# Windowed attention and a two-layer network in split float32: q's and k's parts made over 128 rows and copied into place, the weights' halves added in one step

## The chip, the cores and the metric

The kernel runs on one core of a Trainium2 chip. A core has five engines that run side by side, each with its own queue of instructions: TensorE (PE in the profile; its weight loads are a row of their own, PEld), VectorE (DVE), ScalarE (ACT), GpSimd (POOL) and SyncE (SP), which here only issues DMA transfers. TensorE multiplies a stationary operand, loaded by a weight load, with a moving operand and adds into a bank of PSUM; the other operands lie in SBUF, 128 rows (partitions) wide. The metric is the device time of one execution in microseconds (us), median of several.

## What is computed

The inputs are q, k and v of 8 batches, 8 heads, 576 positions and 64 numbers a head. Each position attends to itself and the 127 positions before it, with a bias that falls with the distance by a slope that depends on the head. The result, 4608 rows of 512, goes through two matrices with a piecewise quadratic function between them. q and k are drawn as normal numbers times 0.8, v times 0.1.

```python
scores = scale * np.matmul(q, k.transpose(0, 1, 3, 2))
rel = pos[:, None] - pos[None, :]
bias = slopes[:, None, None] * (-np.abs(rel))[None, :, :]
mask = (rel >= 0) & (rel < 128)
scores = np.where(mask, scores + bias[None], -1000000000.0)
attn = np.exp(scores - np.max(scores, axis=-1, keepdims=True))
attn = attn / (np.sum(attn, axis=-1, keepdims=True) + 1e-09)
x = np.matmul(attn, v)                       # heads side by side: 4608 x 512
h = x @ w_in                                 # 512 x 2048
g = np.where(h >= 1, h, np.where(h <= -1, 0.0, (h + 1) ** 2 / 4))
out = g @ w_out                              # 2048 x 512
```

## The kernel before

**Split numbers.** Most matmuls run on float32r, a form of float32 with fewer bits. A number is split in two parts: its float32r rounding (high) and the rest (low), and a product is made as high by high, low by high and high by low, all added in one PSUM bank. The copy that rounds is ScalarE's, the subtraction that gives the rest is VectorE's (GpSimd's in the network).

**Chunks, pairs and heads.** The 4608 rows are 12 chunks of 384 (three blocks of 128). In a chunk the 8 heads are taken as 4 pairs, since q and k lie transposed in HBM with two heads of 64 rows on 128 partitions. In the code p counts pairs (48 in all), m heads (96), c chunks. Chunks 0 and 1 are "light" (`LIGHT = 2`): their attention is in plain float32, without splits, and a score is one matmul over the 64 rows of its head (line 288).

**From chunk 2 on.** For a pair, `prepare_k` and `prepare_q` make the operands of the scores. The stationary operand `ql[:, j]` of head j holds q's high part on the head's own 64 rows and its low part on the other 64 (`o_hi`, `o_lo` in lines 241 to 243; one ScalarE and one VectorE step of 64 rows for each head). For that, k's high part must stand on both halves of the rows: `load_qk` brings each head's k from HBM twice, one DMA for each half (line 215), and `prepare_k` splits the doubled k into `kk` (high, line 252) and `kl` (low, line 253), of 128 rows by 2 heads by up to 512 positions. A block of scores is then two matmuls: line 290 multiplies q's high and low parts with k's high part, line 291 the same weights with k's low part, over all 128 rows.

**Softmax.** VectorE adds the table of distances and finds the maximum (line 294), ScalarE takes the exponential and the sum (line 296), VectorE adds up the sums and inverts them (302, 303). A row of scores spans two blocks of keys, 256 wide, of which every column of the left half is masked where the same column of the right half is not; so the two halves are added into 128 columns and multiplied by the inverse in one step for each block (line 309; line 307 where there is no left block). TensorE transposes the 128x128 weights (318). `weights_t` splits them (328, 329), GpSimd parts them again by a triangular mask into the two blocks (331, 333), and `values` multiplies with v's parts (383) and adds up (384 to 387).

**The network.** `layer1` multiplies one of 16 slices of `w_in` with the chunk's x, 12 matmuls of 384 columns into one bank (lines 408 to 410), which ScalarE (417) and VectorE (418, 419) turn into g, split by ScalarE (426) and GpSimd (427). `layer2` follows two slices later with 9 matmuls of 512 columns (441 to 443; 438 in chunk 0, unsplit). The weights arrive as 64-bit floats and are turned into float32 on the chip during the first chunk.

**What sets the order.** The program writes out, step by step, pieces of the attention of chunk c+1 between the steps of the network of chunk c (`segments`, `emit_attention`). A planner then orders every engine's instructions by this order and by its own estimates of when each is ready, places the buffers and makes the waits; each engine works through its queue in that order. Loads of q, k and v, and stores of the output, are issued in order on SP. Most attention buffers exist once (`ql`, `kk`, `kl`, `kr`, `qr`, `z`), so a pair's operands are made after the scores of the pair before it; the weights `ep` exist twice.

Of the kernel before, what the change touches and what calls it, by code (L numbers as in the profile page):

```python
# [8 lines left out]
F32 = mybir.dt.float32  # L9
F32R = mybir.dt.float32r  # L10
I32 = mybir.dt.int32
U32 = mybir.dt.uint32
AF = mybir.ActivationFunctionType
ALU = mybir.AluOpType
# [4 lines left out]
def windowed_attention_then_ffn(  # L19
# [21 lines left out]
    V, S, G, T, DMA = nc.vector, nc.scalar, nc.gpsimd, nc.tensor, nc.sync  # L41

    H, SEQ, D = 8, 576, 64
    NT, DM = out.shape
    DFF = w_in.shape[1]
    P = 128
    NPAIR = H // 2
# [3 lines left out]
    CH = NQB * P  # L51
# [8 lines left out]
    LIGHT = 2  # L60
# [4 lines left out]
    ap1 = ctx.enter_context(tc.tile_pool(name="ap1", bufs=1))  # L65
# [24 lines left out]
    qscale = const.tile([P, NPAIR], F32, name="qscale")  # L90
# [78 lines left out]
    pair = {}  # L169
    head = {}  # L170
    xn = {}
    last_x = [None]
    done_t = {}
    lo_rows = [slice(0, D), slice(D, P)]
    hi_rows = [slice(D, P), slice(0, D)]

    def before(c):

        return 0 if c % CYCLE == 0 else 1

    def load_first(p):

        n = f"_{p}"
        if p == 0:
            qq = [ap1.tile([P, CH], F32, name="qr" + n, tag="qr"), ap1.tile([P, 2, CH], F32, name="ql" + n, tag="ql")[:, 0]]
            kv = [ap1.tile([P, CH + P], F32, name="kr" + n, tag="kr")[:, :CH], ap1.tile([P, CH], F32, name="vn" + n, tag="vn")]
        elif p == 1:
            t = ap1.tile([P, 2, CH], F32, name="qq" + n, tag="kl")
            qq = [t[:, 0], t[:, 1]]
            kv = [ap1.tile([P, CH], F32, name="kr" + n, tag="kk"), ap1.tile([P, CH], F32, name="vn" + n, tag="vs")]  # L190
        else:
            t = wp.tile([P, 2, CH], F32, name="qq" + n, tag=f"wi{NFC - NPAIR + p}")
            qq = [t[:, 0], t[:, 1]]
            t = wp.tile([P, 2, CH], F32, name="kv" + n, tag=f"wo{NFC - NPAIR + p}")
            kv = [t[:, 0], t[:, 1]]
        vn = kv[1].rearrange("p (i j d) -> p i j d", j=2, d=D)
        pair[p] = dict(qr=qq[0], ql=qq[1].rearrange("p (o t) -> p o t", o=1), kr=kv[0].rearrange("p (o t) -> p o t", o=1), vn=vn)
        DMA.dma_start(qq[0], q[p * P:(p + 1) * P, :CH])
        DMA.dma_start(kv[0], k[p * P:(p + 1) * P, :CH])
        DMA.dma_start(vn.rearrange("p i j d -> p i (j d)"), v[:CH, p * P:(p + 1) * P].rearrange("(i p) d -> p i d", p=P))  # L200

    def load_qk(p):

        c, g = divmod(p, NPAIR)
        if c == 0:
            return
        n = CH + before(c) * P
        st = pair[p] = {}
        qr = st["qr"] = ap1.tile([P, CH], F32, name=f"qr_{p}", tag="qr")
        DMA.dma_start(qr, q[g * P:(g + 1) * P, c * CH:(c + 1) * CH])  # L210
        kr = st["kr"] = ap1.tile([P, 2, CH + P], F32, name=f"kr_{p}", tag="kk" if c < LIGHT and p % 2 else "kr")
        if c < LIGHT:
            DMA.dma_start(kr[:, 0, :n], k[g * P:(g + 1) * P, (c + 1) * CH - n:(c + 1) * CH])
            return
        for half in (slice(0, D), slice(D, P)):
            DMA.dma_start(kr[half, :, :n],
                          k[g * P:(g + 1) * P, (c + 1) * CH - n:(c + 1) * CH].rearrange("(j d) t -> d j t", j=2))

    def load_v(p):
        c, g = divmod(p, NPAIR)  # L220
# [11 lines left out]
    def prepare_q(p):  # L232
        qr = pair[p]["qr"]
        if p // NPAIR < LIGHT:
            if p >= NPAIR:
                pair[p]["ql"] = ap1.tile([P, 2, CH], F32, name=f"ql_{p}", tag="ql")
            return S.activation(pair[p]["ql"][:, 0], qr, AF.Copy, scale=qscale[:, p % NPAIR:p % NPAIR + 1])
        ql = pair[p]["ql"] = ap1.tile([P, 2, CH], F32R, name=f"ql_{p}", tag="ql")
        for j in range(2):
            scale = 2.0 ** (2 * (p % NPAIR) + j + 1) / 8.0  # L240
            o_hi, o_lo, s = ql[lo_rows[j], j], ql[hi_rows[j], j], qr[lo_rows[j]]
            S.mul(o_hi, s, scale)
            V.scalar_tensor_tensor(o_lo, s, scale, o_hi.bitcast(F32), ALU.mult, ALU.subtract)

    def prepare_k(p):
        if p // NPAIR < LIGHT:
            return
        n = CH + before(p // NPAIR) * P
        kk = pair[p]["kk"] = ap1.tile([P, 2, CH + P], F32R, name=f"kk_{p}", tag="kk")
        kl = pair[p]["kl"] = ap1.tile([P, 2, CH + P], F32R, name=f"kl_{p}", tag="kl")  # L250
        kr = pair[p]["kr"]
        S.copy(kk[:, :, :n], kr[:, :, :n])
        V.tensor_tensor(kl[:, :, :n], kr[:, :, :n], kk[:, :, :n].bitcast(F32), ALU.subtract)

    def prepare_v(p):
        if p // NPAIR < LIGHT:
# [7 lines left out]
    def scores(m, blks):  # L264
        p, j = divmod(m, 2)
        c = p // NPAIR
        ql, kr, kk, kl = (pair[p].get(x) for x in ("ql", "kr", "kk", "kl"))
        if m not in head:
            head[m] = dict(ep=ap1.tile([P, NQB, P], F32, name=f"ep_{m}", tag="ep", bufs=2),
                           z=wp.tile([P, NQB, 2 * P], F32, name=f"z_{m}", tag=f"wi{NFC - 3}") if c == 0 and j else  # L270
                           ap1.tile([P, NQB, 2 * P], F32, name=f"z_{m}", tag="z"),
                           nmax=ap1.tile([P, 4], F32, name=f"nmax_{m}", tag="nmax", bufs=2),
                           sum=sums[:, m % 2])
        st = head[m]
        nmax, sm, ep, z = st["nmax"], st["sum"], st["ep"], st["z"]
        slope = 2.0 ** -(m % H + 1)
        pt = bank(f"s_{m}_{blks[0]}").rearrange("r (m w) -> r m w", w=2 * P)
        b0 = before(c)
        win = []
        for n, i in enumerate(blks):  # L280
            lone = i + b0 == 0
            c0 = P if lone else D if c % CYCLE == 1 and i == 2 else 0
            k0 = (i + b0 - 1) * P + c0
            o = pt[:, n, c0:]
            win.append((o, c0, lone))
            if c < LIGHT:
                r, qs, ks = lo_rows[j], slice(i * P, (i + 1) * P), slice(k0, k0 + 2 * P - c0)
                st["scored"] = T.matmul(o, ql[r, 0, qs], kr[r, 0, ks], start=True, stop=True).ins  # L288
                continue
            T.matmul(o, ql[:, j, i * P:(i + 1) * P], kk[:, j, k0:k0 + 2 * P - c0], start=True, stop=False)  # L290
            T.matmul(o, ql[:, j, i * P:(i + 1) * P], kl[:, j, k0:k0 + 2 * P - c0], start=False, stop=True)  # L291
        for i, (o, c0, lone) in zip(blks, win):
            r = rel_end if c % CYCLE == 1 and i == 1 else rel
            V.tensor_tensor_reduce(out=z[:, i, c0:], in0=o, in1=r[:, c0:], op0=ALU.add, op1=ALU.min, scale=-slope,  # L294
                                   scalar=3.0e38, accum_out=nmax[:, i:i + 1])
            S.activation(z[:, i, c0:], z[:, i, c0:], AF.Exp, bias=nmax[:, i:i + 1], scale=-1.0,  # L296
                         accum_out=sm[:, i, 0:1])
        if blks[-1] == NQB - 1:
            if c % CYCLE == 1:
                G.memset(z[:, 2, :D], 0.0)  # L300
            rc = st["rc"] = ap1.tile([P, 8], F32, name=f"rc_{m}", tag="rc", bufs=2)
            V.tensor_reduce(rc[:, :NQB], sm, mybir.AxisListType.X, ALU.add)
            V.reciprocal(rc[:, :NQB], rc[:, :NQB])

            for i in range(NQB):
                if i + b0 == 0:
                    V.tensor_tensor(ep[:, i, :], z[:, i, P:], rc[:, i:i + 1].broadcast_to([P, P]), ALU.mult)
                else:
                    st["folded"] = V.tensor_tensor_reduce(out=ep[:, i, :], in0=z[:, i, :P], in1=z[:, i, P:], op0=ALU.add, op1=ALU.add,  # L309
                                           scale=rc[:, i:i + 1], scalar=0.0, accum_out=rc[:, 4 + i:5 + i])  # L310

    def weights_t(m):

# [5 lines left out]
        if m < LIGHT * H:  # L319
            own = lu[:, 0, 1::2, :].bitcast(F32)  # L320
            ga = S.copy(own, pt)
            G.affine_select(out=lu[:, 0, 0::2, :].bitcast(F32), in_=own, pattern=[[0, NQB], [-1, P]],
                            base=0, channel_multiplier=1, compare_op=ALU.is_gt, fill=0.0)
            gg = G.affine_select(out=own, in_=own, pattern=[[0, NQB], [1, P]],
                                 base=0, channel_multiplier=-1, compare_op=ALU.is_ge, fill=0.0)
            done_t[m] = [head[m]["folded"].ins, ga.ins, gg.ins]
            return
        ga = S.copy(lu[:, 0, 1::2, :], pt)
        gv = V.tensor_tensor(lu[:, 1, 1::2, :], pt, lu[:, 0, 1::2, :].bitcast(F32), ALU.subtract)  # L329
# [248 lines left out]
```

## Time and profile before

| | before |
|---|---|
| median of 3 runs | 1066.62 us (1060.73 to 1067.28) |
| the profiled execution | 1068.07 us, of which the span of the instructions is 1066.0 us |
| mean granted clock of TensorE | 0.981 of full speed |
| busy: TensorE, VectorE, ScalarE, GpSimd | 1038.2, 790.1, 618.9, 369.2 us |
| HBM read, written | 58.98 MB, 9.44 MB |

The page of the profile gives each engine's busy time, the chain of work that ended last, and groups of instructions: the line of the kernel, the engine, the operation, output<-inputs with shapes (128x384 is partitions by elements; for matmuls the rows by columns of the array that are used come first, as 64\*128), the count, then the busy time in us and the mean duration in ns, and after the bar the time that the engine stood idle before these instructions and who ended that. A row of waits has who waited for whom, the total in us, how often, and the longest. A row of the timeline has the start in us, the duration in us, the engine, the line and the operation, x the number of neighbours that were merged into it. The records of matmuls overlap: their ends are modelled.

### The profile page before, as it was taken

How to read it: one execution, taken by the hardware profiler on the slowest of the kernel's cores; microseconds unless marked ns; L12 is line 12 of the kernel's file. 1: busy time of each engine (PE TensorE's matmuls, PEld its weight loads, DVE VectorE, ACT ScalarE, POOL GpSimd, SP SyncE). 2: the span in 40 equal slices, each digit the busy share in tenths (PEclk: the TensorE clock that was granted, in tenths of full speed). 3: DMA queues.
4: the chain of work that ended last, by engine and by line, in shares of the span. 5: the costliest groups of instructions: out<-in, count | busy, mean ns of one | idle time of the engine just before them, and what ended most of it. 6: DMA issues, size and time to landing. Idle time of an engine off the chain costs nothing.

```text
span 1066.0 us, 16843 instructions
## 1 busy us (share of the span) xinstructions
PE 1038.2 (97%) x5508; PEld 906.8 (85%) x5508; DVE 790.1 (74%) x2249; ACT 618.9 (58%) x1476; POOL 369.2 (35%) x419
## 2 busy tenths in 40 slices
PE   8999999999999999999999999999999999999998
PEld 5576667998988988998998988999889889899996
DVE  6687799878877788877678887777787897863322
ACT  6687766656556556656456565555555655742322
POOL 2120004444443433433343443433333443333221
PEclk8599999999999999999999999999999999999999
DMA  8346412112212122121113112111121221200000
GB/s 284 100 164 202 136 48 67 53 40 67 65 38 67 48 65 67 41 53 60 36 48 89 43 48 65 62 30 38 60 65 38 77 65 48 67 1 1 31 1 30
DMA packets 58903, 69.50 MB, mean 65 GB/s; under 512 B 4032, under 2 KB 44480, under 8 KB 58816
## 3 DMA queue, kind: packets, MB, share of 16 engines
q1 hardware_dynamic: 48064, 51.66, 17.4%
q10 hardware_dynamic: 10752, 16.78, 4.6%
q8 instruction: 43, 0.70, 0.3%
q14 instruction: 44, 0.36, 0.1%
HBM read 58.98 MB, written 9.44 MB: 64 GB/s over the span
## 4 chain that ended last, share of the span: by engine, by line
PE 85%; DVE 6%; ACT 5%; POOL 2%; issue 2%; DMA 0%; ACTq 0%; SPq 0%; DVEq 0%; POOLq 0%
PE h L408 11%; PE h L409 11%; PE h L410 11%; PE acc L441 11%; PE acc L442 10%; PE acc L443 10%; PE x L383 5%; PE acc L438 3%; PE p L318 3%; PE s L291 2%; PE s L290 2%; PE x L359 2%; PE s L288 2%; ACT z L296 1%; POOL lu L333 1%
## 5 line engine op out<-in xcount | busy, mean ns | idle before, releaser
L427 POOL TENSOR_TENSOR gl<-g,gh 128x384 fp32r<-128x384 f32 x176 | 183.5, 1042 | 435.0 <-ACT gh L426 429.1
L408 PE MATMUL h<-xh,wi 128*128 128x384 f32 x768 | 264.8, 345 | 1.7 <-ACT sg L417 1.7
L409 PE MATMUL h<-xl,wi 128*128 128x384 f32 x768 | 259.8, 338 | 0.0
L410 PE MATMUL h<-xh,wi 128*128 128x384 f32 x768 | 259.4, 338 | 0.0
L441 PE MATMUL acc<-wo,gh 128*128 128x512 f32 x528 | 212.0, 401 | 8.1 <-ACT gh L426 8.1
L418 DVE SCALAR_TENSOR_TENSOR g<-sg 128x384 f32<-128x384 f32 x192 | 108.6, 566 | 148.4 <-ACT sg L417 136.4
L442 PE MATMUL acc<-wo,gh 128*128 128x512 f32 x528 | 208.2, 394 | 0.0
L426 ACT CAST gh<-g 128x384 fp32r<-128x384 f32 x176 | 90.3, 513 | 193.6 <-DVE g L419 179.4
L417 ACT ACTIVATE sg<-h,quarter 128x384 f32<-128x384 f32 x192 | 111.2, 579 | 140.2 <-PE h L410 139.5
L296 ACT ACTIVATE z<-z,nmax 128x256 f32<-128x256 f32 (+2 forms) x288 | 139.0, 485 | 28.5 <-DVE nmax L294 26.6
L443 PE MATMUL acc<-wo,gl 128*128 128x512 f32 x528 | 155.5, 398 | 0.0
L408 PEld LDWEIGHTS h<-xh,wi 128*128 128x128 f32 x768 | 144.6, 188 | 10.7 <-ACT sg L417 3.4
L409 PEld LDWEIGHTS h<-xl,wi 128*128 128x128 f32 x768 | 144.6, 188 | 5.9 <-issue 1.4
L410 PEld LDWEIGHTS h<-xh,wi 128*128 128x128 f32 x768 | 144.4, 188 | 0.0
L294 DVE CUSTOM_DVE_ANT_0 z<-s,rel 128x256 f32<-128x256 f32 (+2 forms) x256 | 94.4, 394 | 51.5 <-PE s L291 44.3
L309 DVE CUSTOM_DVE_ANT_0 ep<-z,rc 128x128 f32<-128x128 f32 x256 | 129.9, 548 | 1.6
L331 POOL TENSOR_SCALAR_AFFINE_SELECT lu<-lu 128x768 fp32r<-128x768 f32 x80 | 80.8, 1010 | 130.2 <-DVE lu L329 121.6
L441 PEld LDWEIGHTS acc<-wo,gh 128*128 128x128 f32 x528 | 99.4, 188 | 27.2 <-ACT gh L426 10.6
L419 DVE SCALAR_TENSOR_TENSOR g<-sg,g 128x384 f32<-128x384 f32 x192 | 112.0, 584 | 3.7
L443 PEld LDWEIGHTS acc<-wo,gl 128*128 128x128 f32 x528 | 97.1, 189 | 19.8 <-POOL gl L427 0.2
L442 PEld LDWEIGHTS acc<-wo,gh 128*128 128x128 f32 x528 | 99.5, 188 | 16.5
L333 POOL TENSOR_SCALAR_AFFINE_SELECT lu<-lu 128x768 fp32r<-128x768 f32 x80 | 81.4, 1018 | 4.6
(88 smaller groups left out, 1461.1 us busy)
## 6 DMA issues: line engine op xcount, KB each, us to landing
kr<-in_k_dram SPq DMA_DIRECT2D x60, 256.0 KB, 4.1
out_dram<-o SPq DMA_DIRECT2D x36, 256.0 KB, 2.4
qr<-in_q_dram SPq DMA_DIRECT2D x45, 192.0 KB, 3.7
rawi<-in_moe_w_in_dram ACTq DMA_DIRECT2D x16, 512.0 KB, 4.6
rawo<-in_moe_w_out_dram ACTq DMA_DIRECT2D x16, 512.0 KB, 5.6
vn<-in_v_dram SPq DMA_DIRECT2D x32, 256.0 KB, 2.8
kr<-in_k_dram SPq DMA_DIRECT2D x26, 192.0 KB, 3.4
vn<-in_v_dram SPq DMA_DIRECT2D x14, 192.0 KB, 2.5
```

The lines of the kernel that those rows point to most:

```text
L296: S.activation(z[:, i, c0:], z[:, i, c0:], AF.Exp, bias=nmax[:, i:i + 1], scale=-1.0, accum_out=sm[:, i, 0:1])
L309: st["folded"] = V.tensor_tensor_reduce(out=ep[:, i, :], in0=z[:, i, :P], in1=z[:, i, P:], op0=ALU.add, op1=ALU.add, scale=rc[:, i:i + 1], ...
L408: T.matmul(ph, wi[fc][:, 0, cc, :], xh, start=(cc == 0), stop=False)
L409: T.matmul(ph, wi[fc][:, 0, cc, :], xl, start=False, stop=False)
L410: T.matmul(ph, wi[fc][:, 1, cc, :], xh, start=False, stop=(cc == NCC - 1))
L417: first = S.activation(sg, ph, AF.Relu, bias=quarter[:, 0:1], scale=0.25)
L418: V.scalar_tensor_tensor(g, sg, 0.5, sg, ALU.min, ALU.mult)
L419: last = V.scalar_tensor_tensor(g, sg, -0.25, g, ALU.add, ALU.max)
L427: G.tensor_tensor(gl, g, gh.bitcast(F32), ALU.subtract)
L441: T.matmul(a, gh[:, ts], wo[fc][:, 0], start=first, stop=False)
L442: T.matmul(a, gh[:, ts], wo[fc][:, 1], start=False, stop=False)
L443: T.matmul(a, gl[:, ts], wo[fc][:, 0], start=False, stop=last)
```

## The change

For q: one ScalarE step multiplies all 128 rows (both heads) by their scales and rounds them into a new tile `qp`; one VectorE step makes the rest, in place of the loaded q. Four DMA copies from SBUF to SBUF, two for each head, then lay the 64-row parts out in `ql` as before.

For k: it is loaded once, in its 128 rows. ScalarE rounds it into `kp[:, 0]`, VectorE writes the rest into `kp[:, 1]`, and four DMA copies bring the high parts into `kk`, each head's on both halves of the rows. The low part stays in its own rows; the matmul of line 291 therefore takes the 64 rows of q's high part alone as its weights, and no longer multiplies q's low part with k's low part.

For the weights: VectorE adds the halves of all blocks in one step in place, and ScalarE multiplies each block by its inverse sums while it writes `ep`.

```diff
@@ load_qk @@
-        kr = st["kr"] = ap1.tile([P, 2, CH + P], F32, name=f"kr_{p}", tag="kk" if c < LIGHT and p % 2 else "kr")
-        if c < LIGHT:
-            DMA.dma_start(kr[:, 0, :n], k[g * P:(g + 1) * P, (c + 1) * CH - n:(c + 1) * CH])
-            return
-        for half in (slice(0, D), slice(D, P)):
-            DMA.dma_start(kr[half, :, :n],
-                          k[g * P:(g + 1) * P, (c + 1) * CH - n:(c + 1) * CH].rearrange("(j d) t -> d j t", j=2))
+        kr = st["kr"] = ap1.tile([P, CH + P], F32, name=f"kr_{p}", tag="kk" if c < LIGHT and p % 2 else "kr")
+        DMA.dma_start(kr[:, :n], k[g * P:(g + 1) * P, (c + 1) * CH - n:(c + 1) * CH])
@@ prepare_q @@
+        scale = qscale[:, p % NPAIR:p % NPAIR + 1]
+        qp = ap1.tile([P, CH], F32R, name=f"qp_{p}", tag="qp")
+        S.activation(qp, qr, AF.Copy, scale=scale)
+        V.scalar_tensor_tensor(qr.bitcast(F32R), qr, scale, qp.bitcast(F32), ALU.mult, ALU.subtract)
         ql = pair[p]["ql"] = ap1.tile([P, 2, CH], F32R, name=f"ql_{p}", tag="ql")
         for j in range(2):
-            scale = 2.0 ** (2 * (p % NPAIR) + j + 1) / 8.0
-            o_hi, o_lo, s = ql[lo_rows[j], j], ql[hi_rows[j], j], qr[lo_rows[j]]
-            S.mul(o_hi, s, scale)
-            V.scalar_tensor_tensor(o_lo, s, scale, o_hi.bitcast(F32), ALU.mult, ALU.subtract)
+            DMA.dma_start(ql[lo_rows[j], j].bitcast(F32), qp[lo_rows[j]].bitcast(F32))
+            DMA.dma_start(ql[hi_rows[j], j].bitcast(F32), qr[lo_rows[j]])
@@ prepare_k @@
+        kr = pair[p]["kr"]
+        kp = ap1.tile([P, 2, CH + P], F32R, name=f"kp_{p}", tag="kl")
+        S.copy(kp[:, 0, :n], kr[:, :n])
+        V.tensor_tensor(kp[:, 1, :n], kr[:, :n], kp[:, 0, :n].bitcast(F32), ALU.subtract)
+        pair[p]["kl"] = kp[:, 1]
+
         kk = pair[p]["kk"] = ap1.tile([P, 2, CH + P], F32R, name=f"kk_{p}", tag="kk")
-        kl = pair[p]["kl"] = ap1.tile([P, 2, CH + P], F32R, name=f"kl_{p}", tag="kl")
-        kr = pair[p]["kr"]
-        S.copy(kk[:, :, :n], kr[:, :, :n])
-        V.tensor_tensor(kl[:, :, :n], kr[:, :, :n], kk[:, :, :n].bitcast(F32), ALU.subtract)
+        for j in range(2):
+            for r in lo_rows:
+                DMA.dma_start(kk[r, j, :n].bitcast(F32), kp[lo_rows[j], 0, :n].bitcast(F32))
@@ scores @@
             T.matmul(o, ql[:, j, i * P:(i + 1) * P], kk[:, j, k0:k0 + 2 * P - c0], start=True, stop=False)
-            T.matmul(o, ql[:, j, i * P:(i + 1) * P], kl[:, j, k0:k0 + 2 * P - c0], start=False, stop=True)
+            T.matmul(o, ql[lo_rows[j], j, i * P:(i + 1) * P], kl[lo_rows[j], k0:k0 + 2 * P - c0], start=False, stop=True)
...
+            n0 = 1 - b0
+            f = V.tensor_tensor(z[:, n0:, P:], z[:, n0:, :P], z[:, n0:, P:], ALU.add)
             for i in range(NQB):
-                if i + b0 == 0:
-                    V.tensor_tensor(ep[:, i, :], z[:, i, P:], rc[:, i:i + 1].broadcast_to([P, P]), ALU.mult)
-                else:
-                    st["folded"] = V.tensor_tensor_reduce(out=ep[:, i, :], in0=z[:, i, :P], in1=z[:, i, P:], op0=ALU.add, op1=ALU.add,
-                                           scale=rc[:, i:i + 1], scalar=0.0, accum_out=rc[:, 4 + i:5 + i])
+                st["folded"] = S.activation(ep[:, i, :], z[:, i, P:], AF.Copy, scale=rc[:, i:i + 1])
+            st["held"] = f
```

Besides, in the light chunks the list of instructions behind which conversions of weights are queued (`done_t`) names the addition instead of the last normalisation.

More of the change, by code (lines that the diff above doesn't have):

```diff
@@ L196, in load_first @@
         vn = kv[1].rearrange("p (i j d) -> p i j d", j=2, d=D)
-        pair[p] = dict(qr=qq[0], ql=qq[1].rearrange("p (o t) -> p o t", o=1), kr=kv[0].rearrange("p (o t) -> p o t", o=1), vn=vn)
+        pair[p] = dict(qr=qq[0], ql=qq[1].rearrange("p (o t) -> p o t", o=1), kr=kv[0], vn=vn)
         DMA.dma_start(qq[0], q[p * P:(p + 1) * P, :CH])
@@ L287, in scores @@
                 r, qs, ks = lo_rows[j], slice(i * P, (i + 1) * P), slice(k0, k0 + 2 * P - c0)
-                st["scored"] = T.matmul(o, ql[r, 0, qs], kr[r, 0, ks], start=True, stop=True).ins
+                st["scored"] = T.matmul(o, ql[r, 0, qs], kr[r, ks], start=True, stop=True).ins
                 continue
             T.matmul(o, ql[:, j, i * P:(i + 1) * P], kk[:, j, k0:k0 + 2 * P - c0], start=True, stop=False)
-            T.matmul(o, ql[:, j, i * P:(i + 1) * P], kl[:, j, k0:k0 + 2 * P - c0], start=False, stop=True)
+            T.matmul(o, ql[lo_rows[j], j, i * P:(i + 1) * P], kl[lo_rows[j], k0:k0 + 2 * P - c0], start=False, stop=True)
         for i, (o, c0, lone) in zip(blks, win):
@@ L325, in weights_t @@
                                  base=0, channel_multiplier=-1, compare_op=ALU.is_ge, fill=0.0)
-            done_t[m] = [head[m]["folded"].ins, ga.ins, gg.ins]
+            done_t[m] = [head[m]["held"].ins, ga.ins, gg.ins]
             return
```

## The prediction

> **What bounds the kernel now.** I read the page first, then the chain of waits, then what TensorE waited for, and last the timeline of TensorE, because a busy share alone cannot say whether its matmuls are closely packed.
>
> ```profile
> span 1066.0 us, 16843 instructions
> PE 1038.2 (97%) x5508; PEld 906.8 (85%) x5508; DVE 790.1 (74%) x2249; ACT 618.9 (58%) x1476; POOL 369.2 (35%) x419
> ...
> PE 85%; DVE 6%; ACT 5%; POOL 2%; issue 2%; DMA 0%; ACTq 0%; SPq 0%; DVEq 0%; POOLq 0%
> ```
>
> TensorE (PE) is busy for 1038.2 of 1066.0 us and carries 85% of the chain that ended last. It is idle for 27.8 us in all, and the two longest causes are these:
>
> ```profile
> PE acc L441 <- ACT gh L426: 8.1, 8, 1.4
> PE x L383 <- POOL lu L333: 6.5, 7, 1.3
> ```
>
> Records of neighbouring matmuls overlap, so I go by the distance from one start to the next. These are three score matmuls of one head (first number: start in us):
>
> ```profile
> 501.74 0.33 PE L290 MATMUL s<-kk,ql 128*128 128x256 f32 x1
> 501.91 0.28 PE L291 MATMUL s<-kl,ql 128*128 128x256 f32 x1
> 502.03 0.28 PE L290 MATMUL s<-kk,ql 128*128 128x256 f32 x1
> ```
>
> L291 takes 0.12 us of TensorE's time (502.03 - 501.91), although its record says 0.28. So TensorE is packed, and the question is what the change does to its own work. Whatever happens on VectorE (DVE, 74%) and ScalarE (ACT, 58%) can win back at most a part of 27.8 us.
>
> **The change on TensorE.** The number of matmuls stays. One form changes: L291, the small half of k against q, now takes 64 rows of weights (one head's rows of q) where it took 128, while its neighbours keep 128. The profile has a column for that shape (128\*128: rows by columns of the array). L291 of before is 128\*128, but the unsplit score matmuls L288 of chunks 0 and 1 are 64\*128, and they stand among 128\*128 matmuls. There one sees what going from one shape to the other costs. Into 64 rows:
>
> ```profile
> 55.20 0.34 PE L409 MATMUL h<-xl,wi 128*128 128x384 f32 x1
> 55.38 0.34 PE L410 MATMUL h<-xh,wi 128*128 128x384 f32 x1
> 55.65 0.48 PE L288 MATMUL s<-kr,ql 64*128 64x256 f32 x1
> ...
> 55.97 0.59 PE L288 MATMUL s<-kr,ql 64*128 64x256 f32 x2
> ...
> 56.18 0.59 PE L288 MATMUL s<-kr,ql 64*128 64x256 f32 x2
> ```
>
> L409 to L410 is 0.18 us, but L410 to L288 is 0.27, so 0.09 us is lost. Then the first L288 takes 0.32 us (55.65 to 55.97) where the next takes 0.21: another 0.11. Out of 64 rows:
>
> ```profile
> 69.25 0.49 PE L288 MATMUL s<-kr,ql 64*128 64x192 f32 x2
> 69.41 0.32 PE L288 MATMUL s<-kr,ql 64*128 64x192 f32 x1
> 69.66 0.19 PEld L408 LDWEIGHTS h<-xh,wi 128*128 128x128 f32 x1 [0.22 <-issue]
> 69.66 0.45 PE L408 MATMUL h<-xh,wi 128*128 128x384 f32 x1
> 69.77 0.19 PEld L409 LDWEIGHTS h<-xl,wi 128*128 128x128 f32 x1
> 69.95 0.34 PE L409 MATMUL h<-xl,wi 128*128 128x384 f32 x1
> ```
>
> The first L288 takes 0.16 us, the second 0.25: 0.09 lost. L408 takes 0.29 (69.66 to 69.95) where a 384-column matmul takes 0.18: 0.11 lost. The weight load (PEld) shows why. It starts only at 69.66 together with the matmul's record, not one matmul earlier, and the following load starts 0.11 us later; so the array first empties (0.09) and then a load that is otherwise hidden stands bare (0.11). I take 0.195 us for each change of shape, a little under the 0.20 of the rounded starts.
>
> How many changes of shape will there be?
>
> ```profile
> L290 PE MATMUL s<-kk,ql 128*128 128x256 f32 (+2 forms) x240 | 67.8, 308 | 0.0
> L291 PE MATMUL s<-kl,ql 128*128 128x256 f32 (+2 forms) x240 | 63.1, 284 | 0.0
> ```
>
> There are 240 of L291. Each closes a sum that an L290 opened, with the next L290, or work of another kind, behind it, so each stands alone: two changes for each, 480 in all. The cost is 480 x 0.195 = 93.6 us, and nothing covers it, because it is TensorE's own time. For a lone 64-row float32r load no row exists. The bare load lies between nothing (then 480 x 0.09 = 43 us are left) and the 0.11 of 64-row L288, which has as many columns and is the nearest row; I take the latter.
>
> A rule of the Trainium skill bears on this. TensorEngine Tiling (Array Packing), Tiling Modes, says that a change of tiling mode drains TensorE; if the drain were all, the cost would be the 43 us just named. The traced rows show the drain and the bare load behind it, so I go by the rows.
>
> **The change on the other engines.** Rows for what goes and for the prices of what comes:
>
> ```profile
> L309 DVE CUSTOM_DVE_ANT_0 ep<-z,rc 128x128 f32<-128x128 f32 x256 | 129.9, 548 | 1.6
> L243 DVE SCALAR_TENSOR_TENSOR ql<-qr,ql 64x384 fp32r<-64x384 f32 x80 | 59.2, 740 | 2.6
> L253 DVE TENSOR_TENSOR kl<-kr,kk 128x1024 fp32r<-128x1024 f32 (+1 forms) x40 | 53.2, 1331 | 2.8 <-ACT kk L252 2.5
> L402 DVE TENSOR_TENSOR xl<-xn,xh 128x384 fp32r<-128x384 f32 x48 | 30.7, 666 | 6.1 <-ACT xh L401 6.1
> L242 ACT ACTIVATE ql<-qr 64x384 fp32r<-64x384 f32 x80 | 41.6, 521 | 1.0
> L252 ACT CAST kk<-kr 128x1024 fp32r<-128x1024 f32 (+1 forms) x40 | 39.4, 985 | 6.8 <-PE s L290 6.1
> L237 ACT ACTIVATE ql<-qr,qscale 128x384 f32<-128x384 f32 x5 | 3.0, 609 | 2.4 <-PE s L288 1.3 <-DMA qr<-in_q_dram 1.1
> ...
> 520.80 0.40 ACT L296 ACTIVATE z<-z,nmax 128x128 f32<-128x128 f32 x1
> ```
>
> VectorE loses L309, L243 and L253, 242.3 us, and gets 96 adds of halves, 40 subtractions for q and 40 for k, at about L402's 0.666 us: 117 us. That leaves some 665 us. ScalarE loses L242 and L252, 81.0 us, and gets 288 normalisations of 128x128 at 0.40 us (the exponential of that size, also with one number per row) and 80 larger ones at about 0.609: 164 us. That makes some 702 us, or 66% of the old span. Neither comes near TensorE. Each head's weights now go VectorE, ScalarE, TensorE instead of VectorE, TensorE. Behind the normalisation in ScalarE's queue stand L417, which empties the bank that the next L408 needs, and L426, for which TensorE already waits 8.1 us. A wait of about one add (0.67 us) there is covered by the layer-2 matmuls between two layer-1 steps; without that cover it would cost up to 96 x 0.67 = 64 us. In the opposite direction, a shorter VectorE queue brings L329 and with it Pool's L333 earlier (6.5 us of idle). I book minus 3 for what these do in the steady part.
>
> In the first chunks the chain runs through the normalisation itself:
>
> ```profile
> 9.51 0.20 DVE ep L307
> ...
> 9.98 0.27 DVE ep L309
> ```
>
> There three steps of 0.2 to 0.3 us become one add (0.67) and three ScalarE steps (0.40 each), about 1.1 us more a head. Few heads are on the chain there, three by my count: plus 3 us.
>
> **The copies.** q and k reach their places by eight copies per pair, issued by SyncE (SP), instead of by ScalarE and VectorE. No copy from SBUF to SBUF is in the trace. The nearest rows are the issues and the time to landing:
>
> ```profile
> 521.01 1.26 SPq L216 DMA_DIRECT2D kr<-in_k_dram  x2
> 522.38 0.52 SPq L210 DMA_DIRECT2D qr<-in_q_dram  x1
> ...
> out_dram<-o SPq DMA_DIRECT2D x36, 256.0 KB, 2.4
> ...
> kr<-in_k_dram SPq DMA_DIRECT2D x60, 256.0 KB, 4.1
> ```
>
> An issue is 0.5 to 0.63 us and a landing 2.4 to 4.1. Eight issues and one landing are 6.4 to 9.1 us after the cast. The old way, and the time until the next pair's first score:
>
> ```profile
> 518.96 0.84 ACT L252 CAST kk<-kr 128x768 fp32r<-128x768 f32 x1
> 521.60 0.55 DVE L243 SCALAR_TENSOR_TENSOR ql<-qr,ql 64x384 fp32r<-64x384 f32 x1
> 525.76 0.31 PE L290 MATMUL s<-kk,ql 128*128 128x128 f32 x1
> ...
> 540.27 0.55 DVE L243 SCALAR_TENSOR_TENSOR ql<-qr,ql 64x384 fp32r<-64x384 f32 x1
> ...
> 542.09 0.36 PE L290 MATMUL s<-kk,ql 128*128 128x256 f32 x1
> ```
>
> Here 3.2 us of preparation were followed by 3.6 us of margin, elsewhere by 1.3 (542.09 - 540.82). So the copies come up to some microseconds later than the old place of the scores. I book nothing for that: layer-1 and layer-2 matmuls are at hand to be placed ahead of the scores, and 40 pairs get 2.3 us each from the changes of shape (93.6 / 40). If that cover is gone, the price is the third rival. Behind a waiting copy on SP stand the loads of the pair after next and the stores of the output; for them nobody waits within a pair's time. HBM reads of k halve, which moves nothing.
>
> **The sum.** The profiled execution took 1068.07 us, 1.45 above the median of 1066.62. 1068.07 + 93.6 - 3 + 3 = 1161.7; less 1.45, rounded: 1160 us.
>
> **Rivals.**
>
> 1. Faster: the change of shape is free where a float32r matmul follows a float32r matmul (all 64-row rows of the trace are plain float32). The skill's page TensorE: Matmul & The Clock Gate, Why this matters for your kernels, says that a matmul of few rows takes the same time as one of 128; by that alone, L291 keeps its 0.12 us. Then only VectorE's relief counts, and with half of TensorE's 27.8 us of idle gone less the 3 us at the start, the time is 1066.6 - 13.9 + 3 = 1056 us. It decides if a change of shape costs under 10.9 / 480 = 0.023 us. Against it stands that L410 and L408, the float32r sides of the rows above, lose as much. Chance 0.05.
> 2. The edit does not take effect as counted: the planner sets two 64-row matmuls side by side, with half the changes, 1066.6 + 46.8 = 1113 us. Against it: an L291 closes the sum of an L290 in the same bank just before it, 0.12 to 0.17 us apart above. Chance 0.06.
> 3. The copies come late, and TensorE stands before the first score of a pair. With 6.4 to 9.1 us against 3.2 + 1.3 to 3.2 + 3.6, the miss is between nothing and 4.6 us a pair; with 1.6 us it is 40 x 1.6 = 64 us more, 1224 us. For it speaks SP's one queue in order, against it the other matmuls at hand. Chance 0.09.
>
> The forecast keeps 0.80; its own range is 1135 (a bare load of half the size: 480 x 0.055 = 26 us less) to 1180 (20 us of new waits). No bare load at all would give 1160 - 50 = 1110, which I count with rival 2. The range 1132 to 1186 leaves out rivals 1 and 2 and most of 3. A measurement of this kernel tells about 1% from no change: faster by more 0.03, within 0.03 (rival 1 lies on that border), slower 0.94.
>
> **What would show it.** L291 with shape 64\*128; a distance of about 0.3 us from an L290 to its L291 and the same back, with the weight load's record starting beside the matmul's; score matmuls taking about 1.2 us more a head (three pairs); VectorE near 665 us, ScalarE near 700; little idle time before L290 that ends with a DMA. I am wrong if the distances stay at 0.12 us, or if TensorE waits for kk or ql.

## The result and the profile after

The changed kernel takes 1132.58 us (1131.52 to 1133.8), the kernel before, on the same chip, 1063.67 (1060.62 to 1067.28): a ratio of 1.0656, with a 95% interval of 1.0624 to 1.0687. The change costs 69 us where 93 were forecast. The profiled execution took 1131.52 us.

First the head of the page of the changed kernel: the span, each engine's busy time, and the chain that ended last.

```profile
span 1129.7 us, 17366 instructions
PE 1111.1 (98%) x5508; PEld 924.6 (82%) x5508; DVE 667.5 (59%) x1761; ACT 676.7 (60%) x1724; POOL 367.0 (32%) x419
...
PE 92%; ACT 3%; DMA 1%; DVE 1%; issue 1%; SPq 1%; POOL 0%; ACTq 0%; DVEq 0%
```

TensorE has the same 5508 matmuls as before and is busy for 73 us more; VectorE is busy for 123 us less, ScalarE for 58 more. TensorE's share of the chain rises from 85% to 92%. Where the time is spent shows in the timeline of TensorE and its weight loads, of which this is a stretch with two score blocks (L293 and L294 are the lines 290 and 291 of before, L443 and L444 layer 2):

```profile
358.13 0.33 PE L412 MATMUL h<-xh,wi 128*128 128x384 f32 x1
358.39 0.18 PEld L294 LDWEIGHTS s<-kp,ql 64*128 64x128 f32 x1 [0.24 <-issue]
358.39 0.38 PE L294 MATMUL s<-kp,ql 64*128 64x256 f32 x1
358.70 0.19 PEld L293 LDWEIGHTS s<-kk,ql 128*128 128x128 f32 x1
358.70 0.39 PE L293 MATMUL s<-kk,ql 128*128 128x256 f32 x1
359.01 0.18 PEld L294 LDWEIGHTS s<-kp,ql 64*128 64x128 f32 x1
359.01 0.38 PE L294 MATMUL s<-kp,ql 64*128 64x256 f32 x1
...
359.33 0.50 PE L443 MATMUL acc<-wo,gh 128*128 128x512 f32 x1
359.43 0.19 PEld L444 LDWEIGHTS acc<-wo,gh 128*128 128x128 f32 x1
359.67 0.39 PE L444 MATMUL acc<-wo,gh 128*128 128x512 f32 x1
```

L294 to L293, L293 to L294 and L294 to L443 are each 0.31 us, where two such score matmuls stood 0.12 apart before: 0.19 lost at each change of shape. Each weight load starts together with its matmul's record instead of one matmul earlier. Behind the last change L443 takes 0.34 (359.33 to 359.67), where layer 2's matmuls usually stand 0.23 apart; this is the bare load again, 0.11, as the next load starts only at 359.43.

For the sums below I took the starts of all TensorE's matmuls in a trace and subtracted from each distance what the same form takes in an undisturbed stretch (float32r: 0.231 us for 512 columns, 0.1745 for 384, 0.117 for 256, and behind a longer matmul 0.089 for 192 and 0.060 for 128; plain float32: 0.429, 0.216 and 0.109 for 512, 256 and 128). What is left at a change of shape I call its cost, the rest lost time: waits, and the slow clock at the start (a granted clock of 0.50 for 34 us of the start in the trace of before). "Network starts" is the start of the first layer-1 matmul. Some 7 us of each span lie ahead of the first matmul and behind the last and are in none of the columns.

| kernel | span | undisturbed work | changes of shape | their cost | lost time | network starts |
|---|---|---|---|---|---|---|
| before | 1066.0 | 986.7 | 58 | 11.2 | 61.2 | 53.9 |
| changed | 1129.7 | 986.7 | 534 | 104.3 | 31.8 | 47.9 |

So 476 more changes cost 93.1 us, 0.196 each, and the lost time fell by 29.4: together 63.7, the difference of the two spans. The medians lie 69 apart, because the time of an execution goes with its granted clock (the kernel before takes 1060 to 1061 us at 0.992, 1067 to 1068 at 0.981), and the traced execution of before had 0.981, that of the changed kernel 0.993. By the medians, then, 24 us of the 93 come back and not 29; in the traces some 25 of the 29.4 fall away after the network has started, some 5 before. The waits of TensorE in the changed kernel show part of the fall; columns as before:

```profile
PE x L361 <- POOL lu L326: 6.7, 5, 3.4
PE acc L443 <- ACT gh L428: 3.0, 3, 1.8
PE p L320 <- ACT ep L311: 2.4, 3, 1.3
PE idle L84 <- POOL qscale L92: 1.6, 1, 1.6
PE h L410 <- ACT sg L419: 0.2, 1, 0.2
```

The waits of values for Pool's mask (6.5 us before, L383 on L333) are gone, those for gh fell from 8.1 to 3.0; those for the mask of the light chunks rose from 2.2 to 6.7 (L359 on L324 before, L361 on L326 here). No row names a DMA: TensorE never stands before kk or ql. The groups of the moved work and the copies:

```profile
L311 ACT ACTIVATE ep<-z,rc 128x128 f32<-128x128 f32 x288 | 94.7, 393 | 21.7 <-DVE rc L306 20.6
L294 PE MATMUL s<-kp,ql 64*128 64x256 f32 (+2 forms) x240 | 89.4, 372 | 0.0
...
L309 DVE TENSOR_TENSOR z<-z 128x384 f32<-128x384 f32 (+1 forms) x96 | 62.7, 653 | 0.0
```

```profile
370.23 2.98 SPq L256 DMA_DIRECT2D kk<-kp  x4
373.25 0.60 SPq L240 DMA_DIRECT2D ql<-qp  x1
...
kk<-kp SPq DMA_DIRECT2D x112, 128.0 KB, 2.4
...
ql<-qp SPq DMA_DIRECT2D x80, 96.0 KB, 2.2
```

A normalisation takes 0.393 us (0.40 was taken from the exponential), an add of halves 0.653 (0.666 taken). Copies land after 2.2 to 2.4 us, and four issues take 2.98 us, some 0.6 for a copy and then the time to the next.

### The profile page after: what moved, and what is told of

The parts are those of the page before. It is cut to its first block, busy times and chain, and to the rows that moved or that the text cites. A ratio compares the mean times of both kernels' runs of the same rounds, so it can differ in the third digit from the quotient of the medians.

```text
span 1129.7 us, 17366 instructions
## 1 busy us (share of the span) xinstructions
PE 1111.1 (98%) x5508; PEld 924.6 (82%) x5508; DVE 667.5 (59%) x1761; ACT 676.7 (60%) x1724; POOL 367.0 (32%) x419
## 4 chain that ended last, share of the span: by engine, by line
PE 92%; ACT 3%; DMA 1%; DVE 1%; issue 1%; SPq 1%; POOL 0%; ACTq 0%; DVEq 0%
PE h L410 12%; PE h L411 11%; PE h L412 11%; PE acc L445 11%; PE acc L443 11%; PE acc L444 11%; PE s L294 6%; PE x L385 5%; PE s L293 4%; PE acc L440 3%; PE p L320 3%; PE x L361 2%; PE s L291 1%; ACT z L299 1%; DMA ql<-qr 1%
## 5 line engine op out<-in xcount | busy, mean ns | idle before, releaser
L429 POOL TENSOR_TENSOR gl<-g,gh 128x384 fp32r<-128x384 f32 x176 | 183.1, 1040 | 384.0 <-ACT gh L428 378.6
L420 DVE SCALAR_TENSOR_TENSOR g<-sg 128x384 f32<-128x384 f32 x192 | 114.1, 594 | 242.7 <-ACT sg L419 224.0
L443 PE MATMUL acc<-wo,gh 128*128 128x512 f32 x528 | 212.2, 402 | 3.0 <-ACT gh L428 3.0
L444 PE MATMUL acc<-wo,gh 128*128 128x512 f32 x528 | 207.7, 393 | 0.0
L333 POOL TENSOR_SCALAR_AFFINE_SELECT lu<-lu 128x768 fp32r<-128x768 f32 x80 | 81.3, 1017 | 236.0 <-DVE lu L331 233.9
L428 ACT CAST gh<-g 128x384 fp32r<-128x384 f32 x176 | 89.9, 511 | 88.3 <-DVE g L421 84.3
L297 DVE CUSTOM_DVE_ANT_0 z<-s,rel 128x256 f32<-128x256 f32 (+2 forms) x256 | 95.1, 394 | 58.5 <-PE s L294 49.5
L443 PEld LDWEIGHTS acc<-wo,gh 128*128 128x128 f32 x528 | 99.4, 188 | 23.1 <-ACT gh L428 4.1
L444 PEld LDWEIGHTS acc<-wo,gh 128*128 128x128 f32 x528 | 99.4, 188 | 15.8
L421 DVE SCALAR_TENSOR_TENSOR g<-sg,g 128x384 f32<-128x384 f32 x192 | 109.6, 571 | 4.3
L445 PEld LDWEIGHTS acc<-wo,gl 128*128 128x128 f32 x528 | 93.5, 188 | 19.4
L311 ACT ACTIVATE ep<-z,rc 128x128 f32<-128x128 f32 x288 | 94.7, 393 | 21.7 <-DVE rc L306 20.6
L294 PE MATMUL s<-kp,ql 64*128 64x256 f32 (+2 forms) x240 | 89.4, 372 | 0.0
```

What stands on the lines that cost most here:

```text
L294: T.matmul(o, ql[lo_rows[j], j, i * P:(i + 1) * P], kl[lo_rows[j], k0:k0 + 2 * P - c0], start=False, stop=True)
L420: V.scalar_tensor_tensor(g, sg, 0.5, sg, ALU.min, ALU.mult)
L421: last = V.scalar_tensor_tensor(g, sg, -0.25, g, ALU.add, ALU.max)
L429: G.tensor_tensor(gl, g, gh.bitcast(F32), ALU.subtract)
L443: T.matmul(a, gh[:, ts], wo[fc][:, 0], start=first, stop=False)
L444: T.matmul(a, gh[:, ts], wo[fc][:, 1], start=False, stop=False)
```

## The experiments

Two theories share the first step, that the changes of shape are the loss, and differ in why the lost time fell: "relief" (VectorE has less to do) and "slack" (TensorE got slower, so what it waits for is ready in time). The rival to both was "copies".

**All 128 rows of weights again, in the changed kernel.** `kp[:, 1]` holds both heads' small halves, so that the matmul can take all rows; q's low part then meets the other head's small half, which adds a product of two low parts:

```diff
-            T.matmul(o, ql[lo_rows[j], j, i * P:(i + 1) * P], kl[lo_rows[j], k0:k0 + 2 * P - c0], start=False, stop=True)
+            T.matmul(o, ql[:, j, i * P:(i + 1) * P], kl[:, k0:k0 + 2 * P - c0], start=False, stop=True)
```

> The changed kernel with one edit: the small half of k against q takes all 128 rows of weights again (q's low part then meets the other head's small half of k, an error of the size of what float32r drops). In the trace of the changed kernel there are 476 more changes of shape on TensorE than the light chunks need, at 0.195 us: 93 us. TensorE's other lost time fell from 61 to 32 us between the two traces. Theory 'shape, and relief': the changes of shape are the whole loss, and the lost time fell because VectorE has less to do: 1132.6 - 93 = 1040 us, faster than the kernel before. Rival 'shape, and slack': the lost time fell only because TensorE itself became slower and everything else came in time; then it comes back: 1040 + 25 = 1065, as before. Rival 'copies': the loss is in copies or queues: it stays near 1132.

Measured: 1049.27 us against 1062.76, a ratio of 0.9855 (0.982 to 0.9891). The instructions stand in the same order on all five engines as in the changed kernel; only the shape differs. Its timeline of TensorE, at the scores of one head:

```profile
346.42 0.36 PE L293 MATMUL s<-kk,ql 128*128 128x256 f32 x1
346.62 0.28 PE L294 MATMUL s<-kp,ql 128*128 128x256 f32 x1
346.73 0.28 PE L293 MATMUL s<-kk,ql 128*128 128x256 f32 x1
346.85 0.28 PE L294 MATMUL s<-kp,ql 128*128 128x256 f32 x1
346.97 0.25 PE L293 MATMUL s<-kk,ql 128*128 128x192 f32 x1
```

Behind the first, which follows a transposition, the distances are back at 0.12. The changes of shape cost 10.3 us (94 less), and 12.8 us of lost time came back (44.6 against 31.8). That falls between the two theories: 1040 was "relief" alone, 1065 "slack" alone. "Copies" falls: with every copy in place the kernel is faster than before.

**64 rows alone, in the kernel before.**

```diff
-            T.matmul(o, ql[:, j, i * P:(i + 1) * P], kl[:, j, k0:k0 + 2 * P - c0], start=False, stop=True)
+            T.matmul(o, ql[lo_rows[j], j, i * P:(i + 1) * P], kl[lo_rows[j], j, k0:k0 + 2 * P - c0], start=False, stop=True)
```

> The kernel before with one edit: the small half of k against q takes 64 rows of weights. (The product of q's low and k's low part is left out, as in the changed kernel.) Theory 'shape, and relief': 480 x 0.195 = 93 us more and the lost time stays: 1157 us. Rival 'shape, and slack': the lost time falls with the slower TensorE by some 25 us: 1132. Rival 'copies': 1064, as before.

Measured: 1134.34 us, a ratio of 1.0667 (1.0626 to 1.0708): as slow as the whole change, with none of its copies and none of its relief. Again all five engines have the same order as the kernel without the edit, so the planner does not see the cost. The changes of shape cost 102.7 us, 91.5 more; the lost time fell from 61.2 to 40.6. TensorE's waits in this kernel:

```profile
PE acc L441 <- ACT gh L426: 4.6, 7, 1.2
PE x L359 <- POOL lu L324: 2.8, 1, 2.8
...
PE x L383 <- POOL lu L333: 0.7, 3, 0.3
```

The waits for gh fell from 8.1 to 4.6, those for the mask from 6.5 to 0.7, though no other engine has less to do. By the medians, too, 20 us of the 91.5 come back. That is "slack".

**The weights' part alone, in the kernel before.** The added and removed lines are those of the change's diff from `n0 = 1 - b0` on.

> The kernel before with the weights' part of the change alone (halves added by VectorE in one step, normalised by ScalarE). VectorE falls by about 100 us, ScalarE rises by about 95. Theory 'relief': TensorE's waits for the GpSimd mask and the network's g shrink, 5 to 20 us less: 1045 to 1060. Rival 'slack': no change, 1064 +- 5.

Measured: 1066.84 against 1062.76 us, a ratio of 1.0025 (1.0005 to 1.0046): VectorE falls from 790.1 to 722.4 us busy, ScalarE rises from 618.9 to 705.2, and it gains nothing. The lost time is 62.1. TensorE's waits in this kernel (lines 440, 407 and 358 are 441, 408 and 359 of before):

```profile
PE acc L440 <- ACT gh L425: 9.1, 11, 2.4
PE h L407 <- ACT sg L416: 4.3, 6, 1.6
PE x L358 <- POOL lu L323: 3.4, 4, 1.2
...
PE x L382 <- POOL lu L332: 1.8, 5, 0.7
```

The waits for the mask fell, 6.5 to 1.8 (L382), as "relief" has it, but those that end with ScalarE rose, 8.1 to 9.1 and 1.7 to 4.3, and so did those of the light chunks, 2.2 to 3.4 (L358). The network starts at 49.5 instead of 53.9.

**q's and k's part alone, with all 128 rows.** The kernel of the first experiment with the weights' part undone.

```diff
-            n0 = 1 - b0
-            f = V.tensor_tensor(z[:, n0:, P:], z[:, n0:, :P], z[:, n0:, P:], ALU.add)
             for i in range(NQB):
-                st["folded"] = S.activation(ep[:, i, :], z[:, i, P:], AF.Copy, scale=rc[:, i:i + 1])
-            st["held"] = f
+                if i + b0 == 0:
+                    V.tensor_tensor(ep[:, i, :], z[:, i, P:], rc[:, i:i + 1].broadcast_to([P, P]), ALU.mult)
+                else:
+                    st["folded"] = V.tensor_tensor_reduce(out=ep[:, i, :], in0=z[:, i, :P], in1=z[:, i, P:], op0=ALU.add, op1=ALU.add,
+                                           scale=rc[:, i:i + 1], scalar=0.0, accum_out=rc[:, 4 + i:5 + i])
```

> The kernel before with q's and k's parts made over 128 rows and laid out by copies, the small half of k against all 128 rows of weights (no change of shape), and the weights as before. Theory 'relief': VectorE falls by about 60 us and ScalarE by about 35, 3 to 12 us less: 1052 to 1061. Rival 'slack': 1064 +- 5. Rival 'copies': the copies land late and TensorE waits for kk or ql, over 1075.

Measured: 1053.71 us, a ratio of 0.9904 (0.987 to 0.9938). Here both VectorE (725.0 us busy) and ScalarE (587.9) have less to do, and the lost time is 49.4. So this part gains some 9 us without any change of shape, as "relief" has it. But the planner also orders these instructions anew, and no run has the shorter work without the new order, so which of the two brings the gain is not shown.

**More work on TensorE without a change of shape, in the kernel before.**

```diff
+            for _ in range(3):
+                T.matmul(o, ql[:, j, i * P:(i + 1) * P], kk[:, j, k0:k0 + 2 * P - c0], start=True, stop=True)
             T.matmul(o, ql[:, j, i * P:(i + 1) * P], kk[:, j, k0:k0 + 2 * P - c0], start=True, stop=False)
```

> The kernel before with one edit: the first score matmul of each block of chunks 2 to 11 is done four times, each time starting its sum anew, so TensorE gets 720 more matmuls of 128 rows and no change of shape. At 0.117 us for 256 columns (0.089 for 192, 0.060 for 128) that is 78 us of added work. Theory 'slack' (TensorE's waits shrink with any added work of its own): 1062.8 + 78 - 20 = 1121 us, with lost time of TensorE falling from 61 to about 40 us. Rival 'the waits shrink only through the changes of shape or through relief of the other engines': 1141 us.

Measured: 1134.64 against 1062.97 us, a ratio of 1.0677 (1.0643 to 1.0711). The expected 78 us of added work were too few: in the trace, one of these matmuls behind another takes 0.119 us at 256 columns and 0.112 at both 192 and 128, which makes 84.7 us. So the lost time fell by 17.0, from 61.2 to 44.2; by the medians 13 us of the 85 are saved. TensorE's waits for gh fell from 8.1 to 0.5, those for the weights of VectorE's L309 rose from 0.2 to 5.3. With 84.7 us "slack" would give 1128 and its rival 1148, and the time lies between them, nearer to "slack". The difference from the 64-row kernel is that this work is known to the planner, which set every engine's order anew around it, while the cost of a change of shape came on top of an order that stayed. That TensorE's running behind its plan is what makes the waits vanish fits both runs, but no run varied that alone.

**Fewer changes of shape, in the changed kernel.** Both blocks that share a bank first with 128 rows, then with 64:

```diff
-            T.matmul(o, ql[:, j, i * P:(i + 1) * P], kk[:, j, k0:k0 + 2 * P - c0], start=True, stop=False)
-            T.matmul(o, ql[lo_rows[j], j, i * P:(i + 1) * P], kl[lo_rows[j], k0:k0 + 2 * P - c0], start=False, stop=True)
+            T.matmul(o, ql[:, j, i * P:(i + 1) * P], kk[:, j, k0:k0 + 2 * P - c0], start=(n == 0), stop=False, skip_group_check=True)
+        for n, (i, (o, c0, lone)) in enumerate(zip(blks, win)):
+            k0 = (i + b0 - 1) * P + c0
+            if c >= LIGHT:
+                T.matmul(o, ql[lo_rows[j], j, i * P:(i + 1) * P], kl[lo_rows[j], k0:k0 + 2 * P - c0], start=False,
+                         stop=(n == len(blks) - 1), skip_group_check=True)
```

> The changed kernel with one edit: of the two blocks that share a bank, first both matmuls of 128 rows, then both of 64 rows, so that a head should have four changes of shape instead of six; the matmuls stay the same. Theory 'price for each change': some 160 changes fewer at 0.195 us, 31 us, of which 3 to 8 come back as waits: 1105 to 1110 us. Rival 'a 64-row matmul is itself slow, whatever stands before it': 1132, as the changed kernel. Rival 'drain alone, 0.09 us a change': 1118 to 1121.

Measured: 1115.41 us, a ratio of 1.0492 (1.0462 to 1.0523). Here is a head in its timeline of TensorE, where the two matmuls of 64 rows (L297) stand side by side:

```profile
343.75 0.48 PE L293 MATMUL s<-kk,ql 128*128 128x256 f32 x2
344.16 0.50 PE L297 MATMUL s<-kp,ql 64*128 64x256 f32 x2
344.59 0.35 PE L293 MATMUL s<-kk,ql 128*128 128x192 f32 x1
344.87 0.35 PE L297 MATMUL s<-kp,ql 64*128 64x192 f32 x1
```

Two matmuls of 64 rows take 0.43 (344.16 to 344.59), which is 2 x 0.117 and one change of shape (0.195). The expected 160 fewer changes were 100 (434 against 534), because the planner put other matmuls between some of them. These 100 cost 20.0 us less, 0.20 each, and 5.9 us of lost time came back; the ratio fell by 0.016, 17 us. With 60 changes more than expected the time is 1115 and not 1105 to 1110, but also not the 1132 of the rival. So the price hangs on the change of shape, not on the 64 rows. 0.09 a change, the drain alone, would have given 9 us.

**An edit meant to change the order.** How far does the planner's order alone move the time? One number in the loop that writes out the attention, once in the kernel before and once in the kernel with all 128 rows:

```diff
-            emit_attention(int(now + (end - now) * (r + (4 if c else 7)) / STEPS))
+            emit_attention(int(now + (end - now) * (r + (5 if c else 7)) / STEPS))
```

> The kernel before with the same work in another order: from chunk 1 on, a chunk's attention is written out one step earlier against the network (5 in place of 4). It tells how far the time moves by the planner's order alone. Theory 'the parts without a change of shape differ only by their plans': this moves by 5 us or more either way. Theory 'relief of VectorE is what the full-row kernel gains': within 4 us of 1063.

> The changed kernel with all 128 rows of weights for the small half of k, and the same other order. Theory 'relief': it keeps its gain, 1045 to 1054 us. Theory 'plans alone': anywhere from 1045 to 1065.

> The changed kernel with all 128 rows of weights, as in the first such run, beside the other order on the same chip: 1049 us, 1.2 to 1.8% under the kernel before.

Measured: the kernel before with this edit 1065.96 us, 1.0029 (1.0006 to 1.0052); all 128 rows with it 1051.51, 0.9895 (0.9861 to 0.9929); all 128 rows as in the first experiment 1051.26, 0.9901 (0.987 to 0.9933), less of a gain than the expected 1.2 to 1.8%. But the edit did not do what it was meant to: in the traces of both kernels the instructions of all five engines stand in the same order as without it. These runs are therefore repeats, and what the order alone is worth stays open. As repeats they show that two sets of runs of one order can lie 0.3% apart, as far as the kernel with the weights' part alone lies from the kernel before, so that 1.0025 is no sure difference. The gain of the kernel with all 128 rows, 1.0 to 1.5%, came in all three sets. It is the fastest kernel of this study, ahead of the kernel before and of the changed one.

The table of the experiments' traces, worked out as above:

| kernel | span | undisturbed work | changes of shape | their cost | lost time | network starts |
|---|---|---|---|---|---|---|
| changed, 128 rows | 1048.5 | 986.7 | 55 | 10.3 | 44.6 | 49.2 |
| before, 64 rows | 1137.0 | 986.7 | 536 | 102.7 | 40.6 | 52.3 |
| before, weights' part | 1066.3 | 986.7 | 55 | 10.5 | 62.1 | 49.5 |
| before, q's and k's part | 1054.6 | 986.7 | 58 | 11.0 | 49.4 | 51.9 |
| before, more matmuls | 1133.6 | 1071.4 | 58 | 11.0 | 44.2 | 51.3 |
| changed, fewer changes | 1115.6 | 986.7 | 434 | 84.3 | 37.7 | 48.8 |

## Why the prediction was right, and where it was off

**The time: in the range by luck.** 1132.58 us lies half a microsecond inside the stated 1132 to 1186 and below the forecast's own 1135 to 1180. The main term was right, and a smaller one was off by nearly as much as the range allowed. Of the 27 us by which 1160 was too high, 3 are the kernel before itself, which took 1063.67 us beside the changed one and not 1066.62.

**The changes of shape: right.** 480 x 0.195 = 93.6 us was the forecast, 476 x 0.196 = 93.1 the trace. The taken bare load for 64-row float32r weights, 0.11 from the plain float32 rows, holds. The rule of the Trainium skill (TensorEngine Tiling (Array Packing), Tiling Modes), that a change of tiling mode drains TensorE, agrees as far as it goes; the measured change costs about twice the drain.

**The lost time: wrong by 24 us by the medians, 29 by the traces.** The step that failed is "I book minus 3 for what these do in the steady part" with the "plus 3 us" at the start. In its place the runs show three things. Some 20 us fall away when TensorE is slower and the order stays (the 64-row kernel, 61.2 to 40.6). Some 12 to 17 in the traces, 9 to 14 by the medians, fall away with q's and k's part and with both parts together (49.4 and 44.6), by the shorter work of the other engines or by the order that the planner makes of it. The two overlap, since a wait that is gone can't go twice: 29.4 together in the traces. I priced relief against the old TensorE and did not ask what the new cost itself does to its idle time. The 27.8 us that I took for the most that could come back was too low as well: a matmul at half clock counts as busy on the page, and lost time by the starts is 61.2.

**The start: wrong sign.** I expected 3 us more from the one add and three ScalarE steps. In the six traces with the weights' part, repeats included, the network starts at 47.9 to 49.8, in the five without it at 51.3 to 53.9: about 3 us less. The clock does not account for that: among the traces with 27 us at a granted clock of 0.50 ahead of it, it starts at 49.5 and 49.8 with the part and at 52.3 and 52.4 without. What on that chain became shorter was not tried.

**The other engines: right in size.** VectorE was put at 665 us and is at 667.5, which is partly luck: L307 (12.1 us) and the reads of the accumulator on L309 (20.3 us) go too and were left out of the sum, while rows overlap, so that taking some away frees less than they add up to. ScalarE was put at 702 us and is at 676.7, mostly because its 288 normalisations are busy for 94.7 us and not 115, neighbours overlapping.

**The copies: right.** Eight issues of about 0.6 us and 2.2 to 2.4 us to landing, and TensorE waits for none of them. q's and k's part with all rows is faster than before.

**The rivals.** The first, a change of shape free among float32r matmuls, falls with the timeline; its rest, relief alone, was put at 1056 us, and the kernel with all 128 rows takes 1049 to 1051. The second, matmuls of 64 rows side by side, did not occur by itself; when written out it took away only 100 of the changes, not 240, and saved 17 us. The third, late copies, falls.

## What to carry to other kernels

Look at the column of shapes before a matmul is cut down: a matmul with fewer rows among full ones is not cheaper, and each change cost 0.195 us here, more than the 0.117 us of the matmul itself. Where rows are to be left out, filling them with something harmless kept both the shape and the gain. A cost that falls on the engine that sets the pace is partly paid out of its own waits, so sum the waits that can vanish before adding the cost in full.

## What was not expected of the hardware

A change of shape cost the same 0.196 us among float32r matmuls as among plain float32 ones, in both directions, wherever both shapes have weights of 128 columns. About 0.09 of it is lost before the new shape starts, which I take for the emptying of the array, and 0.105 behind it, where a weight load stands bare. From SBUF to SBUF, copies of 96 to 128 KB over 64 rows landed 2.2 to 2.4 us after their issue, no later than the 2.5 to 2.9 of the loads of q, k and v from HBM in the same trace (those of the first chunk took 5.4 to 6.7).
